# A fused recurrence, gated feed-forward and routed experts on one core: the load order and the step order ahead of the first block are rewritten

## The chip, the cores and the metric

The kernel runs on one core of one Trainium2 chip, in one launch. Its time is the device time of one execution in microseconds (us), the median of three runs. Engines are named as the profile names them: PE is TensorE (matmul), PEld its weight load, DVE is VectorE, ACT is ScalarE, POOL is GpSimd, SP is SyncE, which here only requests transfers ("DMA").

## The reference

Three stages follow each other. Stage one is a decayed linear recurrence over 768 tokens, for 4 batches of 8 heads of size 48:

```
for t in range(S):
    cur = np.einsum('bhd,bhe->bhde', u[None] * kt, vt)
    y[:, :, t] = np.einsum('bhd,bhde->bhe', rt, state + cur)
    state = w[None, :, :, None] * state + np.einsum('bhd,bhe->bhde', kt, vt)
```

Stage two is a gated feed-forward layer on the 3072 x 384 result: `silu(x @ w_gate) * (x @ w_val) @ w_out`, with an inner size of 1536. Stage three sends each token to one of 8 experts (the largest of 8 logits), runs `relu(h @ w1) @ w2` with an inner size of 1024 there, and scales the row by the router's and an output gate's value.

## The kernel before, in words

The tokens are cut into 24 tiles of 128. Tile i of the program is chunk i // 4 of batch i % 4, so that tiles 0, 1 and 2 are the first chunks of three batches and have no earlier state. Three tiles make a block of 384 tokens; there are 8 blocks. `b_block` runs a block through the feed-forward layer, over 12 slices f of its weights: `b_up` (L498, then silu and product in `b_act`) and, two slices later, `b_down` (L517). The recurrence of the next block's tiles, the conversion of the weights and the routing of the block before are put into `slots` between these matmuls. The experts come last.

Everything stands in a `tc.manual_schedule()`: each engine executes its instructions in the order in which the program issues them, and waits where an operand is not ready. The order of the code is thus the order on each engine, SP included. Every load is requested from SP.

The change lies in the prologue, up to the first `b_up`, and these steps are in it:

- `setup_consts`: zeros and masks; the two loads of the rates w into `wT` (L125).
- `decay_tables` (L155 to L169): a chain of small DVE operations on the rates, which makes the tables `WT` and `pw`.
- `a_load_kr(i)`: keys and receptances of tile i with features on the partitions, into `kr3[i]` (spare11, spare10, spare9), as three loads of 48 partitions: 192 KB and twice 96 KB. `kr3[i]` has been zeroed before. `a_load(i)`: r, k and v of the tile with tokens on the partitions, one load of 576 KB.
- `a_scale(i)` (L322, L324; DVE): the keys and receptances times the tables. `a_scores(i)` (L367; PE): 8 products, 128 x 128 each, into two banks.
- `a_bonus(i)` (L328, L329; POOL): r * u * k in place. `a_diag(i)`: DVE sums it per head (L338), then ACT (tiles 0 and 1, L345, 8 instructions) or POOL (tile 2, L347) writes the sums onto diagonals `at`. `a_mask(i)` (L372; DVE): the scores are copied into `at` above the diagonal.
- `a_out_mm(i)` (PE): `at` times v. Pair 3 of the heads comes first (L394); ACT copies its result to `y3` (L401), which each of the pairs 0 to 2 needs for its own L391.
- `a_out_ev(i)`: the result goes to `xT`, as a high part that ACT casts (L414) and the rest that DVE subtracts (L415).
- `key_table`: a POOL product (L173), four transposes on PE, and a copy on ACT (L176) to `Wk`, which `a_keys` (L356; POOL) needs.
- `conv_steps(f)` (L218 to L220; DVE): float64 weights to float32, by three DVE operations for each of three thirds of 384 columns; the thirds of slice 0 are called step 0, 1 and 2 below. `conv_b`: of the converted weights ACT casts the high part (L236) and POOL subtracts the rest (L237); part `GV` are the first two thirds, `OUT` is the third. `gate_a` (L245 on PE, L247 on ACT) transposes the third one.
- `pe_warm(n)`: n matmuls (L149) whose result nobody reads.

After the prologue comes `conv_a(1)`, the conversion of slice 1 (again 9 DVE operations), and then `b_block(0)`. Its matmuls need all three tiles' `xT` and slice 0's weights. The state copies, scans and memsets named in the code are not needed below.

Of the kernel before, what the change touches and what calls it, by code (L numbers as in the profile page):

```python
# [8 lines left out]
F32 = mybir.dt.float32  # L9
# [42 lines left out]
def kernel(  # L52
# [58 lines left out]
    def bc(ap, axis, shape):  # L111
        return ap.unsqueeze(axis).to_broadcast(shape)
# [4 lines left out]

    def setup_consts():
        dve.memset(wT, 1.0)
        dve.memset(rev, 0.0)  # L120
        act.activation(out=rev, in_=rev, func=AF.Silu)
        dve.memset(kr3[0], 0.0)
        pool.memset(kr3[1], 0.0)
        for j in range(2):
            sp.dma_start(  # L125
                out=wT[64 * j : 64 * j + HD, :],
                in_=w_d.rearrange("(p j) d -> j d p", j=2)[j],
            )
        sp.dma_start(out=ub, in_=u_d.rearrange("h d -> (h d)").partition_broadcast(P))
        make_identity(nc, ident)  # L130
        pool.memset(triu, 1.0)
        pool.affine_select(
            out=triu, in_=triu, compare_op=ALU.is_gt, fill=0.0, base=0,
            pattern=[[1, P]], channel_multiplier=-1,
        )
        pool.tensor_copy(out=mask, in_=triu)
        pool.memset(ones, 1.0)
        pool.memset(cnt, 0.0)
        pool.memset(kr3[2], 0.0)
        pool.memset(spare[4][:, 0 : 6 * P], 0.0)  # L140
        for c in range(KC):
            pool.tensor_copy(
                out=shf[:, c].rearrange("s (j m) -> s j m", j=2)[:, :, HD:64],
                in_=ident.rearrange("s (j m) -> s j m", j=2)[:, :, 16 * c : 16 * c + 16],
            )

    def pe_warm(n, b=7):
        for _ in range(n):
# [19 lines left out]
            dve.tensor_tensor(out=pw[:, :, :, b + 1], in0=pw[:, :, :, b], in1=pw[:, :, :, b], op=ALU.mult)  # L168
        dve.tensor_tensor(out=pw[:, :, :, 7], in0=pw[:, :, :, 6], in1=pw[:, :, :, 6], op=ALU.mult)  # L169

    def key_table():
        wk2 = kp.rearrange("s h d -> s (h d)").rearrange("s (p t) -> s p t", p=4)
        pool.tensor_tensor(out=wk2, in0=WkT, in1=bc(pw[:, 0, :, 7], 2, [P, 4, P]), op=ALU.mult)  # L173
        for p in range(4):
            pe.transpose(bank[7][:, p * P : (p + 1) * P], wk2[:, p, :], ident)
        act.copy(  # L176
            out=Wk.rearrange("s (h d) -> s h d", h=NH),
            in_=bank[7].rearrange("s (h d) -> s h d", h=NH)[:, :, 0:HD],
        )
# [117 lines left out]
    def a_load_kr(i):  # L297
# [7 lines left out]
        else:  # L305
            att.setdefault(i, {}).update({"k": krT[:, 0], "r": krT[:, 1]})
            for j in range(2):
                sp.dma_start(out=krT[64 * j : 64 * j + HD], in_=krT_d[n, j])

    def a_load(i):  # L310
        if i < 3:
            rkv = spare[NF - 4 - i][:, 0 : 3 * DM].rearrange("s (a c) -> s a c", a=3)
        else:
            rkv = apool.tile([P, 3, DM], F32, tag="rkv", name="rkv", bufs=2)
# [493 lines left out]

    with tc.manual_schedule():
        setup_consts()  # L810
        for i in range(3):
            a_load_kr(i)
            a_load(i)
        for f in range(3):
            next_w(f)
        sp.dma_start(out=G, in_=g_d)
        decay_tables()
        for b in range(2):
            pool.memset(Sst[b], 0.0)
        a_bonus(0)  # L820
        a_scale(0)
        a_scores(0, 0)
        a_bonus(1)
        a_scale(1, (0,))
        a_diag(0, True)
        a_scale(1, (1,))
        a_scores(1, 2)
        pe_warm(20)
        a_bonus(2)
        a_scale(2)  # L830
        a_diag(1, True)
        a_mask(0, 0)
        a_out_mm(0, 6, (3,))
        a_scores(2, 4)
        a_diag(2, False)
        a_out_mm(0, 6, (0, 1, 2))
        a_mask(1, 2)
        a_mask(2, 4)
        steps = conv_steps(0)
        a_out_ev(0, 6)  # L840
        steps[0]()
        a_out_mm(1, 0, (3,))
        key_table()
        a_out_mm(2, 1, (3,))
        a_out_mm(1, 0, (0, 1, 2))
        steps[1]()
        a_out_mm(2, 1, (0, 1, 2))
        steps[2]()
        a_out_ev(1, 0)
        pool.memset(krT, 0.0)  # L850
        for i in range(3):
            a_keys(i)
        for b in (2, 3):
            pool.memset(Sst[b], 0.0)
        conv_b(0, (GV,))
# [261 lines left out]
def _layout(inputs):  # L1117
# [21 lines left out]
    for i, name in enumerate(("moe_w_gate", "moe_w_val")):  # L1139
# [8 lines left out]
    return {  # L1148
        "krT": np.ascontiguousarray(np.stack([feat(inputs["k"]), feat(inputs["r"])], axis=3)),
        "rkv": np.ascontiguousarray(np.stack([tok(inputs[n]) for n in "rkv"], axis=2)),  # L1150
        "w": np.ascontiguousarray(inputs["w"]), "u": np.ascontiguousarray(inputs["u"]),
        "w64": w64, "g": g, "w12": w12,
    }

# [20 lines left out]
```

## Time and profile before

| | |
|---|---|
| time, three runs | 858.78 us median (857.08 to 859.10) |
| the profiled execution | 857.18 us, of which the span is 855.5 us |
| busy share of the span | PE 96%, PEld 93%, DVE 54%, ACT 32%, POOL 31% |
| granted TensorE clock over the span, as a share of 2.4 GHz | 0.993 |
| HBM traffic over the span | 120 GB/s |

The shares are means over stages that differ. In the first fortieth of the span (21.4 us) the page gives PE 4 tenths and DVE 7, in the second PE 9 and DVE 8. What a change of the prologue is worth is therefore read from the prologue's own rows and from the chain of waits behind it, not from the shares. In the rows below a line number is that of the kernel before.

### The profile page before, as it was taken

How to read it: one execution, taken by the hardware profiler on the slowest of the kernel's cores; microseconds unless marked ns; L12 is line 12 of the kernel's file. 1: busy time of each engine (PE TensorE's matmuls, PEld its weight loads, DVE VectorE, ACT ScalarE, POOL GpSimd, SP SyncE). 2: the span in 40 equal slices, each digit the busy share in tenths (PEclk: the TensorE clock that was granted, in tenths of full speed). 3: DMA queues.
4: the chain of work that ended last, by engine and by line, in shares of the span. 5: the costliest groups of instructions: out<-in, count | busy, mean ns of one | idle time of the engine just before them, and what ended most of it. 6: DMA issues, size and time to landing. Idle time of an engine off the chain costs nothing.

```text
span 855.5 us, 13963 instructions
## 1 busy us (share of the span) xinstructions
PE 824.2 (96%) x5472; PEld 793.4 (93%) x5472; DVE 459.5 (54%) x945; ACT 271.2 (32%) x590; POOL 265.4 (31%) x241
## 2 busy tenths in 40 slices
PE   4988899999999999999999999999999999999996
PEld 3768789999999999999999999999999999999996
DVE  7888764344465455456455444234565566466541
ACT  2334342212211221222222222223454444444432
POOL 6755564233334425244244112010110211021022
PEclk9989999999999999999999999999999999999999
DMA  8815415843333322323323210410494544435201
GB/s 225 303 53 188 154 61 138 238 127 117 102 111 100 122 79 89 117 87 125 114 102 130 61 48 29 162 51 1 140 349 142 170 140 140 157 123 167 82 26 36
DMA packets 29769, 104.90 MB, mean 123 GB/s; under 512 B 5175, under 2 KB 14193, under 8 KB 26624
## 3 DMA queue, kind: packets, MB, share of 16 engines
q1 hardware_dynamic: 26368, 94.37, 34.4%
q0 software_dynamic: 3328, 9.56, 3.0%
q8 instruction: 45, 0.74, 0.4%
q14 instruction: 28, 0.23, 0.1%
HBM read 85.84 MB, written 16.41 MB: 120 GB/s over the span
## 4 chain that ended last, share of the span: by engine, by line
PE 87%; DVE 7%; issue 2%; DMA 1%; ACT 1%; SPq 1%; POOL 0%; POOLq 0%; DVEq 0%; ACTq 0%
PE bank L498 33%; PE bank L517 17%; PE bank L714 12%; PE bank L731 12%; PE bank L367 3%; PE bank L394 2%; PE bank L380 2%; DVE bank L219 2%; DVE bank L218 2%; DVE cv L220 1%; PE bank L679 1%; PE bank L745 1%; DMA spare<-in_krT_dram 1%; PE bank L431 1%; DVE s L507 0%
## 5 line engine op out<-in xcount | busy, mean ns | idle before, releaser
L498 PE MATMUL bank<-xT,W 128*128 128x384 f32 x1728 | 330.8, 341 | 1.1 <-DMA xT<-stage 0.9
L498 PEld LDWEIGHTS bank<-xT,W 128*128 128x128 f32 x1728 | 304.9, 189 | 5.2 <-DMA xT<-stage 1.5
L517 PE MATMUL bank<-W,h 128*128 128x400 f32 x864 | 174.6, 346 | 0.0
L517 PEld LDWEIGHTS bank<-W,h 128*128 128x128 f32 x864 | 154.7, 188 | 0.4 <-DVE h L510 0.2
L509 ACT CAST h<-s 128x384 fp32r<-128x384 f32 x96 | 49.2, 513 | 325.0 <-DVE s L507 325.0
L507 DVE TENSOR_TENSOR s<-s,bank 128x384 f32<-128x384 f32 x96 | 53.2, 554 | 158.1 <-PE bank L498 145.2
L731 PE MATMUL bank<-hd,wf 128*128 128x416 f32 (+1 forms) x576 | 113.8, 344 | 0.0
L731 PEld LDWEIGHTS bank<-hd,wf 128*128 128x128 f32 x576 | 104.3, 188 | 0.7 <-DVE hd L718 0.2
L753 POOL DMA_INDIRECT out_dram<-yo,ix x32 | 34.2, 1067 | 201.4 <-DVE yo L749 175.1
L347 POOL TENSOR_TENSOR at<-ident,a 128x1024 f32<-128x1024 f32 x19 | 36.0, 1896 | 149.0 <-PE bank L498 118.0
L510 DVE TENSOR_TENSOR h<-s,h 128x384 fp32r<-128x384 f32 x84 | 52.9, 630 | 48.6 <-ACT h L509 48.6
L718 DVE SCALAR_TENSOR_TENSOR hd<-bank,hd 128x416 fp32r<-128x416 f32 (+1 forms) x64 | 36.7, 573 | 77.0 <-ACT hd L717 77.0
L663 DVE TENSOR_TENSOR wf<-raw,wf 128x768 fp32r<-128x768 f32 x64 | 61.2, 957 | 7.0 <-ACT wf L662 1.2
L506 ACT ACTIVATE s<-bank 128x384 f32<-128x384 f32 x96 | 47.2, 492 | 46.8 <-PE bank L498 46.8
L579 POOL DMA_INDIRECT xs<-rows,slot x24 | 23.7, 988 | 112.9 <-DVE slot L577 51.5
L717 ACT ACTIVATE hd<-bank 128x416 fp32r<-128x416 f32 (+1 forms) x64 | 32.3, 505 | 82.3 <-PE bank L714 81.9
L714 PE MATMUL bank<-xd1h,wf 128*128 128x416 f32 x192 | 58.3, 361 | 0.0
L662 ACT CAST wf<-raw 128x768 fp32r<-128x768 f32 x64 | 52.8, 825 | 0.0
L372 DVE COPY_PREDICATED at<-mask,bank 128x512 f32<-128x512 int32 x42 | 28.6, 733 | 38.2 <-POOL at L347 35.3
L714 PE MATMUL bank<-xd0h,wf 128*128 128x416 f32 x144 | 43.8, 362 | 0.0
L714 PEld LDWEIGHTS bank<-xd1h,wf 128*128 128x128 f32 x192 | 36.0, 188 | 0.5
L328 POOL TENSOR_TENSOR rkv<-rkv,ub 128x384 f32<-128x384 f32 x21 | 21.3, 1016 | 48.6 <-DMA rkv<-in_rkv_dram 48.6
(177 smaller groups left out, 951.5 us busy)
## 6 DMA issues: line engine op xcount, KB each, us to landing
raw<-in_w_dram SPq DMA_DIRECT2D x36, 768.0 KB, 4.4
raw<-in_w_dram SPq DMA_DIRECT2D x22, 1152.0 KB, 7.2
rkv<-in_rkv_dram SPq DMA_DIRECT2D x21, 576.0 KB, 5.4
krT<-in_krT_dram SPq DMA_DIRECT2D x42, 192.0 KB, 3.4
xs<-zt SPq DMA_DIRECT2D x32, 197.0 KB, 5.8
xr<-xs SPq DMA_DIRECT2D x6, 591.0 KB, 5.7
spare<-in_w_dram SPq DMA_DIRECT2D x2, 1152.0 KB, 9.6
xT<-stage SPq DMA_DIRECT2D x42, 48.0 KB, 2.1
```

Of the source, the lines that this page charges most:

```text
L347: pool.tensor_tensor(out=af, in0=bc(ident, 1, [P, NH, P]), in1=bc(a, 2, [P, NH, P]), op=ALU.mult)
L498: pe.matmul(ps[i], W[f][:, wl, o : o + P], x[:, xl, c, :], start=(c == 0 and n == 0), stop=(c == KC - 1 and n == 2),)
L506: act.activation(out=s, in_=g, func=AF.Silu)
L507: dve.tensor_tensor(out=s, in0=s, in1=v, op=ALU.mult)
L509: act.copy(out=h[:, 0], in_=s)
L510: (pool if blk == 0 else dve).tensor_tensor(out=h[:, 1], in0=s, in1=h[:, 0].bitcast(F32), op=ALU.subtract)
L517: pe.matmul(bank[t][:, 0 : DM + 16], h[:, hl, t * P : (t + 1) * P], W[f][:, wl, 2 * KC * P :], start=(f == 0 and n == 0), stop=(f == NF - ...
L662: act.copy(out=wf[:, 0], in_=raw[:, f])
L663: dve.tensor_tensor(out=wf[:, 1], in0=raw[:, f], in1=wf[:, 0].bitcast(F32), op=ALU.subtract)
L714: pe.matmul(ps, wf[:, wl, c * P : (c + 1) * P], xd[xl][:, c, 0:n], start=(i == 0), stop=(i == 3 * KC - 1))
L718: dve.scalar_tensor_tensor(h[:, 1, 0:n], ps, 0.0, h[:, 0, 0:n].bitcast(F32), ALU.max, ALU.subtract)
L731: pe.matmul(bank[c][:, 0:n], wf[:, wl, o : o + P], h[:, hl, 0:n], start=(f == 0 and i == 0), stop=(f == NEF - 1 and i == 2),)
```

## The change

Loads. The rates come from a second input that the host lays out as 2 x 48 x 4, so that a partition's four values lie together. All nine loads of keys and receptances of tiles 0, 1 and 2 are requested before u and before anything with tokens on the partitions; then r and k of the three tiles (384 KB each, `a_load_part`), weight slice 0, v of the three tiles (192 KB each), slices 1 and 2, and the rest as before.

Zeros. The zeros of `kr3[2]` move from POOL to DVE, ahead of the decay tables; the zeros of two states move ahead of the bonuses on POOL.

Order of the steps. The three bonuses come first, then POOL's product for the key table; the scores of all three tiles are issued before the first `a_out_mm`; 8 dummy matmuls stand in place of 20. The first third of slice 0 is converted before tile 0's `a_out_ev`, the second before tile 1's, the third before tile 2's; `conv_b(GV)` is issued before tile 1's `a_out_ev`, and `gate_a` before tile 2's. The zeros of `krT`, `a_keys` and the last two states' zeros come behind all of this.

```
     def setup_consts():
         dve.memset(wT, 1.0)
+        for j in range(2):
+            sp.dma_start(out=wT[64 * j : 64 * j + HD], in_=wt_d[j])
+        dve.memset(kr3[0], 0.0)
         dve.memset(rev, 0.0)
         act.activation(out=rev, in_=rev, func=AF.Silu)
-        dve.memset(kr3[0], 0.0)
+        a_load_kr(0)
         pool.memset(kr3[1], 0.0)
-        for j in range(2):
-            sp.dma_start(
-                out=wT[64 * j : 64 * j + HD, :],
-                in_=w_d.rearrange("(p j) d -> j d p", j=2)[j],
-            )
-        sp.dma_start(out=ub, in_=u_d.rearrange("h d -> (h d)").partition_broadcast(P))
+        dve.memset(kr3[2], 0.0)
...
-        pool.memset(kr3[2], 0.0)
...
+    def a_load_part(i, lo, hi):
+        t = spare[NF - 4 - i][:, lo * DM : hi * DM].rearrange("s (a c) -> s a c", a=hi - lo)
+        sp.dma_start(out=t, in_=rkv_d[a_tile(i)][:, lo:hi])
+        att[i].update({"rkv"[n] + "n": t[:, n - lo] for n in range(lo, hi)})
...
         setup_consts()
+        a_load_kr(1)
+        a_load_kr(2)
+        sp.dma_start(out=ub, in_=u_d.rearrange("h d -> (h d)").partition_broadcast(P))
         for i in range(3):
-            a_load_kr(i)
-            a_load(i)
-        for f in range(3):
-            next_w(f)
+            a_load_part(i, 0, 2)
+        next_w(0)
+        for i in range(3):
+            a_load_part(i, 2, 3)
+        next_w(1)
+        next_w(2)
         sp.dma_start(out=G, in_=g_d)
         decay_tables()
-        for b in range(2):
-            pool.memset(Sst[b], 0.0)
-        a_bonus(0)
+        for i in range(3):
+            a_bonus(i)
+        key_table_a()
         a_scale(0)
         a_scores(0, 0)
-        a_bonus(1)
-        a_scale(1, (0,))
+        a_scale(1)
+        a_scores(1, 2)
         a_diag(0, True)
-        a_scale(1, (1,))
-        a_scores(1, 2)
-        pe_warm(20)
-        a_bonus(2)
         a_scale(2)
+        a_scores(2, 4)
+        pe_warm(8)
         a_diag(1, True)
         a_mask(0, 0)
         a_out_mm(0, 6, (3,))
-        a_scores(2, 4)
         a_diag(2, False)
+        a_mask(1, 2)
+        key_table_b()
+        a_out_mm(1, 0, (3,))
         a_out_mm(0, 6, (0, 1, 2))
-        a_mask(1, 2)
         a_mask(2, 4)
-        steps = conv_steps(0)
-        a_out_ev(0, 6)
-        steps[0]()
-        a_out_mm(1, 0, (3,))
-        key_table()
         a_out_mm(2, 1, (3,))
         a_out_mm(1, 0, (0, 1, 2))
+        steps = conv_steps(0)
+        steps[0]()
+        a_out_ev(0, 6)
         steps[1]()
+        conv_b(0, (GV,))
         a_out_mm(2, 1, (0, 1, 2))
+        a_out_ev(1, 0)
         steps[2]()
-        a_out_ev(1, 0)
+        gate_a(0)
+        a_out_ev(2, 1)
+        conv_b(0, (OUT,))
         pool.memset(krT, 0.0)
         for i in range(3):
             a_keys(i)
         for b in (2, 3):
             pool.memset(Sst[b], 0.0)
-        conv_b(0, (GV,))
-        a_out_ev(2, 1)
-        gate_a(0)
-        conv_b(0, (OUT,))
```

SP's requests from the third on, before (spare11, 10 and 9 hold the keys of tiles 0, 1 and 2; spare8, 7 and 6 hold their r, k and v):

```order
L129 DMA ub_75<-in_u_dram 128x384
L302 DMA spare11_104<-in_krT_dram 48x1024
L303 DMA spare11_104<-in_krT_dram 48x512
L304 DMA spare11_104<-in_krT_dram 48x512
L315 DMA spare8_101<-in_rkv_dram 128x1152
L302 DMA spare10_103<-in_krT_dram 48x1024
L303 DMA spare10_103<-in_krT_dram 48x512
L304 DMA spare10_103<-in_krT_dram 48x512
L315 DMA spare7_100<-in_rkv_dram 128x1152
L302 DMA spare9_102<-in_krT_dram 48x1024
L303 DMA spare9_102<-in_krT_dram 48x512
L304 DMA spare9_102<-in_krT_dram 48x512
```

The same place in the changed kernel:

```order
L305 DMA spare11_104<-in_krT_dram 48x1024
L306 DMA spare11_104<-in_krT_dram 48x512
L307 DMA spare11_104<-in_krT_dram 48x512
L305 DMA spare10_103<-in_krT_dram 48x1024
L306 DMA spare10_103<-in_krT_dram 48x512
L307 DMA spare10_103<-in_krT_dram 48x512
L305 DMA spare9_102<-in_krT_dram 48x1024
L306 DMA spare9_102<-in_krT_dram 48x512
L307 DMA spare9_102<-in_krT_dram 48x512
L818 DMA ub_75<-in_u_dram 128x384
L315 DMA spare8_101<-in_rkv_dram 128x768
L315 DMA spare7_100<-in_rkv_dram 128x768
```

The keys of tiles 1 and 2 have moved ahead of u and of every load with tokens on the partitions.

DVE from the first scaling on, before (a is the sum for the diagonal of a tile, bank0 and bank1 hold tile 0's scores):

```order
L322 TENSOR_TENSOR spare11_104<-spare11_104,WT_73 128x1024
L324 TENSOR_TENSOR spare11_104<-spare11_104,WT_73 128x512
L322 TENSOR_TENSOR spare10_103<-spare10_103,WT_73 128x1024
L338 TENSOR_REDUCE a_195<-spare8_101 128x4x2
L324 TENSOR_TENSOR spare10_103<-spare10_103,WT_73 128x512
L322 TENSOR_TENSOR spare9_102<-spare9_102,WT_73 128x1024
L324 TENSOR_TENSOR spare9_102<-spare9_102,WT_73 128x512
L338 TENSOR_REDUCE a_238<-spare7_100 128x4x2
L372 COPY_PREDICATED spare8_101<-mask_70,bank0_61 128x512
L372 COPY_PREDICATED spare8_101<-mask_70,bank1_62 128x512
```

The same place in the changed kernel:

```order
L327 TENSOR_TENSOR spare11_104<-spare11_104,WT_73 128x1024
L329 TENSOR_TENSOR spare11_104<-spare11_104,WT_73 128x512
L327 TENSOR_TENSOR spare10_103<-spare10_103,WT_73 128x1024
L329 TENSOR_TENSOR spare10_103<-spare10_103,WT_73 128x512
L343 TENSOR_REDUCE a_210<-spare8_101 128x4x2
L327 TENSOR_TENSOR spare9_102<-spare9_102,WT_73 128x1024
L329 TENSOR_TENSOR spare9_102<-spare9_102,WT_73 128x512
L343 TENSOR_REDUCE a_238<-spare7_100 128x4x2
L377 COPY_PREDICATED spare8_101<-mask_70,bank0_61 128x512
L377 COPY_PREDICATED spare8_101<-mask_70,bank1_62 128x512
```

Tile 1's scaling is no longer cut in two by tile 0's sum; tile 2's stands behind that sum in both kernels.

ACT from the first copy of pair 3 on (bank6, bank0 and bank1 hold the outputs of tiles 0, 1 and 2; cv is slice 0 converted, W0 its parts, gt its transposed third), before:

```order
L401 COPY spare4_97<-bank6_67 48x128 x2
L414 CAST xT_279<-bank6_67 128x3x128
L401 COPY spare4_97<-bank0_61 48x128 x2
L176 COPY Wk_74<-bank7_68 128x384
L401 COPY spare4_97<-bank1_62 48x128 x2
L414 CAST xT_279<-bank0_61 128x3x128
L236 CAST W0_331<-cv_278 128x768
L414 CAST xT_279<-bank1_62 128x3x128
L247 COPY gt_339<-bank7_68 128x384
L236 CAST W0_331<-cv_278 128x384
```

The same place in the changed kernel:

```order
L406 COPY spare4_97<-bank6_67 48x128 x2
L179 COPY Wk_74<-bank7_68 128x384
L406 COPY spare4_97<-bank0_61 48x128 x2
L406 COPY spare4_97<-bank1_62 48x128 x2
L419 CAST xT_296<-bank6_67 128x3x128
L239 CAST W0_302<-cv_292 128x768
L419 CAST xT_296<-bank0_61 128x3x128
L250 COPY gt_322<-bank7_68 128x384
L419 CAST xT_296<-bank1_62 128x3x128
L239 CAST W0_302<-cv_292 128x384
```

The cast of tile 1's output now stands behind the cast of slice 0's first two thirds, and that of tile 2's behind the copy of the transposed third; tile 0's stands behind the copies of pair 3 of all three tiles.

## Rows read from the trace of the kernel before

**Rows 1.** Chain of waits, 25 to 130 us; columns: start us, us, what.

```profile
26.88 0.56 DVE bank L218
...
31.62 0.55 DVE cv L220
...
72.56 2.65 PE bank L498 x9
...
77.51 1.60 PE bank L498 x9
...
111.66 0.56 DVE s L507
```

**Rows 2.** Timeline of DVE; columns: start us, us, instruction, [idle before <-releaser].

```profile
3.50 2.35 DVE L155 TENSOR_SCALAR pw<-wT 128x4 f32<-128x4 f32 x1 [0.81 <-DMA wT<-in_w_dram]
...
9.61 1.22 DVE L322 TENSOR_TENSOR spare<-spare,WT 128x1024 f32<-128x1024 f32 x1
...
13.03 1.40 DVE L322 TENSOR_TENSOR spare<-spare,WT 128x1024 f32<-128x1024 f32 x1 [1.61 <-DMA spare<-in_krT_dram]
14.36 0.54 DVE L338 TENSOR_REDUCE a<-spare 128x8 f32<-128x384 f32 x1
...
17.72 1.23 DVE L322 TENSOR_TENSOR spare<-spare,WT 128x1024 f32<-128x1024 f32 x1 [2.22 <-DMA spare<-in_krT_dram]
...
24.08 1.34 DVE L372 COPY_PREDICATED spare<-mask,bank 128x512 f32<-128x512 int32 x2 [0.76 <-POOL spare L347]
26.40 0.56 DVE L415 TENSOR_TENSOR xT<-bank,xT 128x384 fp32r<-128x384 f32 x1 [0.99 <-ACT xT L414]
...
33.02 0.55 DVE L218 TENSOR_SCALAR bank<-raw 128x384 int32<-128x384 int32 x1
```

**Rows 3.** Timeline of POOL.

```profile
15.63 1.00 POOL L328 TENSOR_TENSOR spare<-spare,ub 128x384 f32<-128x384 f32 x1 [2.28 <-DMA spare<-in_rkv_dram]
16.71 1.00 POOL L329 TENSOR_TENSOR spare<-spare 128x384 f32<-128x384 f32 x1
...
22.15 1.90 POOL L347 TENSOR_TENSOR spare<-ident,a 128x1024 f32<-128x1024 f32 x1 [0.67 <-DVE a L338]
24.00 1.05 POOL L173 TENSOR_TENSOR kp<-WT,pw 128x512 f32<-128x512 f32 x1
```

**Rows 4.** Timeline of SP (a row is a request).

```profile
8.23 0.42 SPq L304 DMA_DIRECT2D spare<-in_krT_dram  x1
```

**Rows 5.** Busy time and DMA by stretch; columns: stretch, length, busy (instructions) of each engine, granted clock, DMA share, GB/s.

```profile
15.00:17.00 2.00, 1.74 (x9) 1.45 (x8) 0.49 (x1) 2.00 (x8) 1.29 (x2) 1.00 1.07 214
18.00:20.00 2.00, 2.00 (x14) 1.22 (x13) 2.00 (x4) 0.00 (x0) 1.09 (x1) 1.00 1.00 417
...
44.00:46.00 2.00, 0.21 (x2) 0.21 (x3) 1.91 (x6) 0.81 (x4) 0.26 (x1) 1.00 0.16 58
...
48.00:50.00 2.00, 2.00 (x9) 2.00 (x9) 1.86 (x4) 0.77 (x3) 2.00 (x1) 0.50 0.00 0
```

**Rows 6.** Timeline of ACT.

```profile
20.04 2.45 ACT L345 ACTIVATE spare<-ident,a 128x128 f32<-128x128 f32 x8 [2.67 <-DVE a L338]
...
27.20 0.53 ACT L401 COPY spare<-bank 48x128 f32<-48x128 f32 x2
29.37 0.48 ACT L414 CAST xT<-bank 128x384 fp32r<-128x384 f32 x1 [1.65 <-PE bank L394]
30.43 0.83 ACT L236 CAST W<-cv 128x768 fp32r<-128x768 f32 x1 [0.57 <-DVE cv L220]
...
32.81 0.48 ACT L247 COPY gt<-bank 128x384 f32<-128x384 f32 x1 [0.64 <-PE bank L245]
```

**Rows 7.** Timeline of PE.

```profile
30.03 0.49 PE L391 MATMUL bank<-spare 128*128 128x128 f32 x2
...
31.22 0.43 PE L394 MATMUL bank<-spare 128*48 128x128 f32 x4
...
32.23 0.55 PE L245 MATMUL bank<-ident,cv 128*128 128x128 f32 x3 [0.58 <-DVE cv L220]
```

More of the change, by code (lines that the diff above doesn't have):

```diff
@@ L57 @@
     w_d: bass.AP,
+    wt_d: bass.AP,
     u_d: bass.AP,
@@ L145, in setup_consts @@
             )
+        for b in range(2):
+            pool.memset(Sst[b], 0.0)
     def pe_warm(n, b=7):
@@ L169, in decay_tables, with key_table_a, key_table_b @@
         dve.tensor_tensor(out=pw[:, :, :, 7], in0=pw[:, :, :, 6], in1=pw[:, :, :, 6], op=ALU.mult)
-    def key_table():
-        wk2 = kp.rearrange("s h d -> s (h d)").rearrange("s (p t) -> s p t", p=4)
+    wk2 = kp.rearrange("s h d -> s (h d)").rearrange("s (p t) -> s p t", p=4)
+    def key_table_a():
         pool.tensor_tensor(out=wk2, in0=WkT, in1=bc(pw[:, 0, :, 7], 2, [P, 4, P]), op=ALU.mult)
+    def key_table_b():
         for p in range(4):
@@ L308, in a_load_kr @@
                 sp.dma_start(out=krT[64 * j : 64 * j + HD], in_=krT_d[n, j])
+    def a_load_part(i, lo, hi):
+        t = spare[NF - 4 - i][:, lo * DM : hi * DM].rearrange("s (a c) -> s a c", a=hi - lo)
+        sp.dma_start(out=t, in_=rkv_d[a_tile(i)][:, lo:hi])
+        att[i].update({"rkv"[n] + "n": t[:, n - lo] for n in range(lo, hi)})
     def a_load(i):
[L311 to L314, printed above, removed]
+        rkv = apool.tile([P, 3, DM], F32, tag="rkv", name="rkv", bufs=2)
         sp.dma_start(out=rkv, in_=rkv_d[a_tile(i)])
@@ L1150, in _layout @@
         "rkv": np.ascontiguousarray(np.stack([tok(inputs[n]) for n in "rkv"], axis=2)),
-        "w": np.ascontiguousarray(inputs["w"]), "u": np.ascontiguousarray(inputs["u"]),
+        "w": np.ascontiguousarray(inputs["w"]),
+        "wt": np.ascontiguousarray(np.asarray(inputs["w"]).reshape(4, 2, HD).transpose(1, 2, 0)),
+        "u": np.ascontiguousarray(inputs["u"]),
         "w64": w64, "g": g, "w12": w12,
```

## Prediction

> **What bounds the kernel now.** I read the chain of waits first, since it tells on which engine the start of the program costs time. From 26.88 us on it runs on DVE, conversion after conversion, and it is still on DVE at 111.66 us [rows 1]. In between it leaves DVE for short pieces on PE, ACT and POOL, each of which follows from a DVE result. So the first block is paced by DVE until about 112 us, and PE only after that. A DVE chain that begins later by x makes the program longer by x, unless one of the short pieces absorbs it. I therefore look for one number: when does DVE begin slice 1's conversion? Now that is at 33.02 us [rows 2]. All that the change does ends ahead of that instruction, and the work behind it keeps its order on every engine but POOL and SP, of which below.
>
> Next I read DVE's timeline ahead of it [rows 2]. The last mask ends at 24.08 + 1.34 = 25.42 us. DVE then waits 0.99 us for tile 0's cast, and from 26.40 us on it does not wait again: tile 0's rest, three conversion steps (26.88 to 32.17 us [rows 1], 1.76 us each), the rests of tiles 1 and 2, slice 1. Ahead of the last mask DVE waits for transfers (1.61 us and 2.22 us for keys [rows 2], POOL 2.28 us for a token tile [rows 3]).
>
> **The loads.** Until 17 us they move at 214 GB/s, from 18 us on at 417 [rows 5]. A key tile (384 KB, three loads of 48 partitions) adds 2.1 us to the stream: tile 1's token load is there at 15.63 us [rows 3], tile 2's keys at 17.72 us [rows 2]. Tile 0's keys are all there by 8.2 us, since SP's request at 8.23 us no longer waits for them [rows 4]. With u (192 KB, about 0.5 us at 417 GB/s) no longer ahead, I take 7.7 us for them, then 9.8 and 11.9 us for tiles 1 and 2. Behind them come u and r, k of tile 0, 590 kB: 1.4 us at 417 GB/s. So r and k of tile 0 land at about 13.3 us, which I call R. Both ends: if the key tiles are held only by SP's requests (0.42 us each [rows 4], say 1.4 us a tile with gaps), R = 7.7 + 2.8 + 1.4 = 11.9 us; if the token loads also go at 214 GB/s, 2.75 us in place of 1.4, R = 14.6 us. I take 13.3 us because a key tile's 2.1 us is measured and nothing of a key load is mixed in any more behind 11.9 us.
>
> The Trainium skill (SBUF — State Buffer, Door 1: The DMA port swizzle) says that a load onto partitions 0 to 47 reaches only 8 of 16 ports, about 218 GB/s at most. The measured 2.1 us for 393 kB is 187 GB/s, of that size; by the page alone a key tile would take 1.8 us, R would be 12.7 us and the sum below 0.6 us smaller. That rule speaks against putting all the slow loads first, since what waits for tokens then stands behind 1.2 MB of them.
>
> Slice 0 (1180 kB) and v follow r, k of three tiles: even v of tile 2 is there by R + 786/417 + 1180/417 + 590/417 = R + 6.1, about 19.4 us, ahead of its use. Fewer packets for the rates bring them at most the 0.81 us earlier that DVE waited for them [rows 2], and DVE is zeroing then. Both cost and gain nothing, as the next paragraph shows; without that cover they would be worth that 0.81 us.
>
> **The steps up to the last mask.** POOL now has three bonuses in a row, 2.08 us each (15.63 to 17.71 us [rows 3]), then the table product (1.05 us) and tile 2's diagonal (1.90 us) [rows 3]; then DVE's last mask (1.34 us [rows 2]). With 0.1 us of gaps the last mask ends at R + 6.25 + 1.05 + 1.90 + 1.34 + 0.1 = R + 10.65, 23.95 us: a gain of 1.5 us at this place. Is DVE ready for it? The second zeroing on DVE, L155 (2.35 us for four columns [rows 2], held by something that the row does not name) and the tables end no later than about 11.1 us (9.61 us now [rows 2], and 1.5 us for a zeroing, an estimate from the width). Two tiles' scalings (1.23 us and about half of it again [rows 2]) end by 14.9 us, before tile 0's bonus at R + 2.1 = 15.4 us lets the first sum go. So anything from a gain of 2.35 us to a loss of 1.5 us there is hidden by the wait for R; without that wait it would shift the masks one for one. The moved zeros on POOL fall before R as well.
>
> Tile 1's mask matters too, for PE waits for it: R + 2.1, sum 0.54 [rows 2], tile 0's diagonal on ACT 2.45, tile 1's 2.45 [rows 6], mask 1.34, 0.1 of gaps: M = R + 9.0 = 22.3 us. The scores of tile 2 (and 8 dummies for 20) lie ahead of this on PE, which is otherwise idle there.
>
> **From there to slice 1.** Here the new order costs. ACT and PE keep program order, and three hand-overs are now in series with DVE's steps, where before only one (0.99 us [rows 2]) was. From M:
>
> - PE: pair 3 of tile 1 (0.43), three pairs of tile 0 (0.81 each: 30.03 to 31.65 us is two), pair 3 of tile 2 (0.43) [rows 7]: M + 3.3. ACT: copies of pair 3 (0.53), then tile 0's cast (0.48) [rows 6]: M + 4.35. DVE finished step 0 at 23.95 + 1.76 = 25.7 us, M + 3.4, and waits about 0.95 us. Its rest for tile 0 takes 0.48 us (26.40 to 26.88 us): M + 4.85.
> - Step 1: M + 6.6. Only then can ACT cast the first two thirds of the slice (0.83 us), and tile 1's cast (0.48 us [rows 6]) stands behind it in ACT's queue: DVE waits 1.35 us for what PE had ready long before. Rest of tile 1: M + 8.45.
> - Step 2: M + 10.2. Now PE transposes the third (0.55 us [rows 7]), ACT copies it (0.48 us), and tile 2's cast (0.48 us [rows 6]) stands behind that copy: DVE waits 1.55 us. Rest of tile 2: M + 12.3.
>
> Slice 1 begins at M + 12.3 = 34.6 us, against 33.02 us: **later by 1.6 us**. The first block's first matmuls need tile 2's cast too and move by about the same. The waits that come (0.95 + 1.35 + 1.55 = 3.85 us, against 0.99 us) outweigh the head's gain. By R's bounds the sum goes from +0.2 us (R = 11.9) to +2.9 us (R = 14.6).
>
> Moved behind on POOL: the zeros of krT, the three key products and two zeros come after slice 0's last rest, from about 36 to 42 us. Queued behind them are tile 3's bonus and slice 1's rest, for which PE's matmuls of slice 1 wait. In the trace PE stands nearly idle from 44 to 46 us (0.21 us busy in 2 [rows 5]) because DVE is behind, so up to some 2 us on PE there is hidden; without that cover it would be 1 to 2 us. SP keeps the later slices' requests behind krT's; slice 3 is converted only in the stretch from 48 us on, and I cost it at nothing.
>
> Against the profiled execution's own 857.18 us (span 855.5) the sum is 858.8 us. That execution lies 1.6 us under the median of the three runs, 858.78 us, so the forecast on the median's scale is **860.4 us**. About 0.3%, 2.6 us, is what a measurement of this kernel can tell from no change.
>
> **Rivals.**
>
> *The features come early and the head wins.* Mechanism: the nine key loads, with nothing mixed in, are limited by SP's requests alone, and R is below 11.7 us, the point from which the sum turns negative. At best DVE's scalings bound the first sum: tables at 8.3 us (1.3 us earlier), two scalings to 12.1 us, then 0.54 + 2.45 + 2.45 + 1.34 + 0.1 = M at 19.0 us and slice 1 at 31.3 us, 1.7 us earlier: 857.1 us. For: the rate from 18 us on. Against: the 2.1 us per key tile. Chance 0.17; faster by over 0.3% only if also the half clock below happens to fall away.
>
> *PE falls to its lower clock in the new gap.* After tile 2's last pair, near M + 8, PE has only three transposes until M + 11.8. In the trace PE was 0.21 us busy from 44 to 46 us, and from 48 to 50 us the granted clock is 0.50, the 1.2 GHz level [rows 5]. Nine matmuls then take 2.65 us against 1.60 us [rows 1]. The first 18 matmuls at that level would be 2.1 us longer, and what follows on PE some more. It decides only where PE's slack behind DVE (about 2 us, above) is used up: with the 1.6 us, 862.5 us. The Trainium skill (TensorE: Matmul & The Clock Gate, What's actually happening) makes the lower clock the state that an idle PE falls back to; the rows of 44 to 50 us agree. Chance 0.23.
>
> *The shift is absorbed.* At 72.56 us the chain lies on nine matmuls at the lower clock [rows 1]. If the later start moves PE's gaps so that this stretch runs at 2.4 GHz, 1.05 us and a little for the transposes come back: 859.1 us, no difference. Chance 0.15.
>
> The forecast itself, with R between the bounds and the chain carried through: 0.45, from 859.0 to 861.7 us.
>
> **How the numbers follow.** Forecast and absorbed shift lie within 0.3% but for the upper end of R (0.07 of slower). The early features lie within it for 0.11 and beyond for 0.06. The clock rival is slower for 0.19 and the same for 0.04. Together: faster 0.06, same 0.68, slower 0.26. The range, 857.5 to 863.0 us, reaches down to 1.3 us under the median of before, into the early features, and up to 4.2 us over it, past the clock rival.
>
> **What would show it.** Right: slice 1's first conversion at 34 to 36 us; DVE idle about 1.4 us ahead of tile 1's rest, released by ACT, and 1.5 us ahead of tile 2's; the last mask near 24 us; POOL's first bonus near 13 us; the DVE chain unbroken to about 112 us. Wrong: the first bonus before 11.7 us, slice 1 before 33 us, or a chain that leaves DVE before 60 us for good.

## The result and the profile after

The changed kernel takes 863.22 us (median of 4 runs, 862.00 to 864.13) against 858.94 us (4 runs, 857.08 to 859.93) for the kernel before, run beside it: ratio 1.0054, 95% interval 1.0037 to 1.0071. It is slower by about 4.3 us. The profiled execution took 862.92 us, its span is 861.1 us, the mean granted clock 0.990.

DVE's timeline of the changed kernel (start, us, instruction, idle time before it and what ended it; line numbers are now 5 higher), to be held against [rows 2]:

```profile
15.37 0.56 DVE L343 TENSOR_REDUCE a<-spare 128x8 f32<-128x384 f32 x1 [3.52 <-POOL spare L334]
15.84 1.53 DVE L327 TENSOR_TENSOR spare<-spare,WT 128x1024 f32<-128x1024 f32 x1
17.29 1.48 DVE L329 TENSOR_TENSOR spare<-spare,WT 128x512 f32<-128x512 f32 x1
...
21.22 1.33 DVE L377 COPY_PREDICATED spare<-mask,bank 128x512 f32<-128x512 int32 x2
23.61 1.34 DVE L377 COPY_PREDICATED spare<-mask,bank 128x512 f32<-128x512 int32 x2 [1.06 <-POOL spare L352]
...
28.27 0.56 DVE L420 TENSOR_TENSOR xT<-bank,xT 128x384 fp32r<-128x384 f32 x1 [1.53 <-ACT xT L419]
...
31.75 0.56 DVE L420 TENSOR_TENSOR xT<-bank,xT 128x384 fp32r<-128x384 f32 x1 [1.28 <-ACT xT L419]
...
35.49 0.56 DVE L420 TENSOR_TENSOR xT<-bank,xT 128x384 fp32r<-128x384 f32 x1 [1.53 <-ACT xT L419]
35.97 0.55 DVE L221 TENSOR_SCALAR bank<-raw 128x384 int32<-128x384 int32 x1
```

Slice 1 begins at 35.97 us, 2.95 us later than before. The three waits ahead of the rests are there, 1.53, 1.28 and 1.53 us. POOL's timeline beside it [rows 3]:

```profile
13.26 1.00 POOL L333 TENSOR_TENSOR spare<-spare,ub 128x384 f32<-128x384 f32 x1 [7.24 <-DMA spare<-in_rkv_dram]
...
16.37 1.86 POOL L334 TENSOR_TENSOR spare<-spare 128x384 f32<-128x384 f32 x1
18.19 1.44 POOL L333 TENSOR_TENSOR spare<-spare,ub 128x384 f32<-128x384 f32 x1
19.71 1.00 POOL L334 TENSOR_TENSOR spare<-spare 128x384 f32<-128x384 f32 x1
```

The bonus products of 1.00 us take 1.86 and 1.44 us where DVE scales tile 2, and the second part of that scaling takes 1.48 us, against 0.68 us for tile 0 at 9.43 us. PE's timeline [rows 7]:

```profile
18.83 3.16 PE L372 MATMUL bank<-spare 128*128 128x128 f32 x14 [0.92 <-DVE spare L329]
21.83 1.46 PE L149 MATMUL bank<-ones 128*128 128x384 bf16 x8
...
24.16 0.42 PE L399 MATMUL bank<-spare 128*48 128x128 f32 x4
...
34.02 0.55 PE L248 MATMUL bank<-ident,cv 128*128 128x128 f32 x3 [2.25 <-DVE cv L223]
35.52 5.02 PE L503 MATMUL bank<-xT,W 128*128 128x384 f32 x18 [0.95 <-ACT xT L419]
...
59.05 0.80 PE L248 MATMUL bank<-ident,cv 128*128 128x128 f32 x3 [3.26 <-DVE at L377]
...
61.71 3.35 PE L522 MATMUL bank<-W,h 128*128 128x400 f32 x9
```

Tile 1's mask ends at 22.55 us, but its pair 3 runs only at 24.16 us. The scores of tile 2 and the 8 dummies lie ahead of it, end 0.74 us behind the mask (21.83 + 1.46 = 23.29 us), and are followed by tile 0's pair 3 and the key table's transposes, 0.94 us together, ahead of tile 1. Busy times by stretch, columns as in [rows 5], show the granted clock:

```profile
18.00:22.00 4.00, 3.17 (x16) 3.09 (x17) 3.74 (x7) 2.85 (x10) 3.92 (x5) 0.57 1.03 426
...
34.00:38.00 4.00, 3.03 (x10) 2.49 (x11) 2.40 (x5) 1.27 (x3) 2.05 (x3) 0.66 0.00 0
...
62.00:66.00 4.00, 4.00 (x13) 3.97 (x13) 2.09 (x4) 0.73 (x3) 1.19 (x3) 0.50 0.19 34
```

PE stands at 1.2 GHz in three stretches (from 18.2, 35.3 and 59.2 us), each behind a wait. The last one lies on the path. The chain of waits of the changed kernel there (L512 is the silu product on DVE):

```profile
57.18 0.56 DVE s L512
...
60.41 1.46 PE bank L256 x6
61.87 3.19 PE bank L522 x9
65.06 2.10 PE bank L503 x9
67.26 0.57 DVE s L512
...
116.67 0.56 DVE s L512
```

and the same pieces of the kernel before:

```profile
54.23 0.55 DVE s L507
...
57.23 0.84 PE bank L253 x6
58.07 1.73 PE bank L517 x9
59.80 1.60 PE bank L498 x9
61.50 0.56 DVE s L507
```

From the first of these products to the second it took 7.27 us and takes 10.08 us. So the chain is 2.95 us late up to 57.18 us and 5.76 us late at 67.26 us. Then it gets 0.75 us back, since the half-clock stretch that lay on the path before (72.56 us in [rows 1]) has gone, and stands at 5.01 us at 116.67 us. There is 0.6 us more by the end of the span.

### The profile page after: what moved, and what is told of

Same layout as the page of the kernel before. It is cut to its first block, busy times and chain, and to the rows that moved or that the text cites. A ratio compares the mean times of both kernels' runs of the same rounds, so it can differ in the third digit from the quotient of the medians.

```text
span 861.1 us, 13942 instructions
## 1 busy us (share of the span) xinstructions
PE 823.8 (96%) x5460; PEld 793.2 (92%) x5460; DVE 458.3 (53%) x946; ACT 270.8 (31%) x590; POOL 266.7 (31%) x240
## 4 chain that ended last, share of the span: by engine, by line
PE 82%; DVE 7%; issue 5%; ACT 2%; POOL 1%; DMA 1%; SPq 0%; POOLq 0%; DVEq 0%
PE bank L503 32%; PE bank L522 17%; PE bank L719 11%; PE bank L736 11%; PE bank L372 3%; PE bank L399 2%; PE bank L385 2%; DVE bank L222 2%; DVE bank L221 2%; DVE cv L223 1%; PE bank L684 1%; PE bank L750 1%; DMA spare<-in_rkv_dram 1%; PE bank L436 1%; POOL W L240 1%
## 5 line engine op out<-in xcount | busy, mean ns | idle before, releaser
L522 PE MATMUL bank<-W,h 128*128 128x400 f32 x864 | 176.0, 348 | 0.0
L522 PEld LDWEIGHTS bank<-W,h 128*128 128x128 f32 x864 | 155.9, 189 | 0.4 <-DVE h L515 0.2
L512 DVE TENSOR_TENSOR s<-s,bank 128x384 f32<-128x384 f32 x96 | 53.2, 554 | 161.6 <-PE bank L503 148.5
L515 DVE TENSOR_TENSOR h<-s,h 128x384 fp32r<-128x384 f32 x84 | 50.7, 603 | 48.6 <-ACT h L514 48.6
L377 DVE COPY_PREDICATED at<-mask,bank 128x512 f32<-128x512 int32 x42 | 28.5, 732 | 38.2 <-POOL at L352 35.3
```

Of the source, the lines that this page charges most:

```text
L512: dve.tensor_tensor(out=s, in0=s, in1=v, op=ALU.mult)
L515: (pool if blk == 0 else dve).tensor_tensor(out=h[:, 1], in0=s, in1=h[:, 0].bitcast(F32), op=ALU.subtract)
L522: pe.matmul(bank[t][:, 0 : DM + 16], h[:, hl, t * P : (t + 1) * P], W[f][:, wl, 2 * KC * P :], start=(f == 0 and n == 0), stop=(f == NF - ...
```

## The experiments

The kernel before ran beside them on the same chip; its medians in the four sessions were 858.61, 858.60, 858.91 and 858.32 us. Each run has 7 to 12 executions, and the one whose trace is shown lies up to 2.8 us from the median of its run (e2 856.88 us, e4 863.09 us), so a trace tells where time goes in one execution, and the table what the edit is worth. "Tail" means the steps from the first `conv_steps` on.

| run | edit | median us | ratio to before, 95% |
|---|---|---|---|
| e1 | before + new tail | 862.30 | 1.0030 to 1.0059 |
| e2 | after, rests not in series | 859.70 | 0.9999 to 1.0028 |
| e3 | before + new loads, zeros | 861.21 | 1.0012 to 1.0040 |
| e4 | after + 18 dummies ahead of slice 3's transposes | 860.58 | 1.0010 to 1.0036 |
| e5 | after, tile 2 scaled early | 860.07 | 1.0001 to 1.0028 |
| e6 | e2 and e5 together | 857.70 | 0.9981 to 1.0006 |
| e7 | e6 + the 18 dummies | 855.98 | 0.9959 to 0.9987 |
| e8 | e3 + 16 dummies ahead of tile 1's scores | 859.13 | 0.9993 to 1.0019 |
| e9 | after + 16 dummies ahead of tile 2's scores | 861.33 | 1.0021 to 1.0048 |
| e10 | e9 + the 18 dummies | 859.51 | 1.0002 to 1.0024 |
| e11 | after, the last hand-over undone | 860.82 | 1.0021 to 1.0049 |
| e12 | e7 with the old load order | 859.67 | 1.0006 to 1.0028 |
| e13 | after, POOL's zeros and keys early | 862.54 | 1.0033 to 1.0067 |
| e14 | e6, POOL's zeros and keys early | 855.72 | 0.9954 to 0.9980 |
| e15 | e7, POOL's zeros and keys early | 857.75 | 0.9981 to 1.0005 |

**The halves of the change apart: the tail (e1), the loads (e3), the rests out of series (e2).** e1 is the kernel before with the tail of the changed one (POOL's zeros and keys late too), but with `key_table` and the out-products where they were. e3 has only the new loads and zeros. e2:

```
         steps[1]()
-        conv_b(0, (GV,))
         a_out_mm(2, 1, (0, 1, 2))
-        a_out_ev(1, 0)
         steps[2]()
-        gate_a(0)
+        a_out_ev(1, 0)
+        conv_b(0, (GV,))
         a_out_ev(2, 1)
+        gate_a(0)
         conv_b(0, (OUT,))
```

> The kernel before with only the new order of the tail of the prologue (conversion steps, casts, transposes, late zeros); loads and scores as before. Theory S (the hand-overs to ACT and PE that stand in series with DVE's conversion steps): slice 1's conversion begins at about 35.1 us instead of 33.0, DVE waits about 1.3 us ahead of tile 1's rest and 1.5 us ahead of tile 2's, and the time is about 861 us, 2.1 over before. Rival C (the loss comes from stretches at TensorE's lower clock that the new head brings): slice 1's start moves by 2 us too, but the time stays within 1 us of before unless a new stretch at half clock shows. Rival L (the load order): no difference, 859 us.

> The changed kernel with tile 1's rest behind the third conversion step and tile 2's cast ahead of the transposes, so that two of the three hand-overs leave DVE's path; all else as changed. Theory S: DVE still waits about 1.5 us ahead of tile 0's rest, then no more; slice 1 begins at about 33.3 us instead of 36.0, and the time is about 2.7 us under the changed kernel, 860.5 us, if the clock's stretches stay as they are. Rival C: slice 1 begins 2.7 us earlier, but the time follows the half-clock stretches: 860 to 863 us. Rival L: no difference to the changed kernel, 863 us.

> The kernel before with only the new loads (keys first, r and k, slice 0, v, rates in few packets) and the moved zeros of the third key tile; the order of all steps as before. Theory S: the first bonus begins at about 13.3 us, the last mask ends at about 24 us, slice 1 begins at 32 to 33 us, time 857.5 to 859 us. Rival L: slice 1 begins later than 33.5 us, and the time is 2 us or more over before.

The tail alone costs 3.7 us on the kernel before, more than the 2.1 us expected: slice 1 starts at 36.17 us, behind waits of 1.43, 1.28 and 1.89 us, and PE is at half clock around 36 and 62 us there too. Taking the series out of the changed kernel gives back 3.5 us. DVE in e2:

```profile
26.08 0.56 DVE L420 TENSOR_TENSOR xT<-bank,xT 128x384 fp32r<-128x384 f32 x1 [0.21 <-ACT xT L419]
...
29.98 1.01 DVE L420 TENSOR_TENSOR xT<-bank,xT 128x384 fp32r<-128x384 f32 x2
30.91 0.55 DVE L221 TENSOR_SCALAR bank<-raw 128x384 int32<-128x384 int32 x1
```

Two of the three waits are gone, the third is 0.21 us, and slice 1 starts 2.1 us ahead of the kernel before, 2.4 us earlier than was expected (in a profile with the first bonus at 12.39 us and the clock at 1.0 throughout the prologue). So the head of the change does gain for DVE, and the series takes more than that. The time does not follow: e2's median is 1.1 us over the kernel before, which its interval does not tell from no change. e3 was a surprise: the loads alone cost 2.6 us, although its first bonus came at 13.49 us, about as in the changed kernel. PE in e3:

```profile
17.11 3.35 PE L367 MATMUL bank<-spare 128*128 128x128 f32 x14 [3.70 <-DVE spare L324]
20.26 4.73 PE L147 MATMUL bank<-ones 128*128 128x384 bf16 x20
```

PE waits 3.70 us for tile 1's second scaling, which stands behind the first sum on DVE. Its clock then falls to 0.50 from 16.1 to 22.9 us, and the scores of tile 2, behind the dummies, end too late for the last mask (27.21 us, after 3.09 us of waiting for PE; 24 us was expected). That led to the runs with dummies.

**PE's clock: e4 (ahead of slice 3's transposes), e8 and e9 (in the prologue), e10 (both).**

```
                     slots[2 * f - 3 + (f == 3)].insert(0, lambda f=f: gate_a(f))
+                    if f == 3: slots[4].insert(0, lambda: pe_warm(18, 0))
...
         a_scale(2)
+        pe_warm(16)
         a_scores(2, 4)
```

The first is e4, the second e9. e8 has `pe_warm(16)` ahead of `a_scores(1, 2)` in e3.

> The changed kernel with 18 dummy matmuls into a free bank where PE is idle from 55.8 to 59.0 us, ahead of slice 3's transposes; nothing else changed. Theory S with the clock as its multiplier: slice 1 still begins at 36.0 us, the granted clock from 59 to 66 us is 1.00 instead of 0.50, the third silu product comes at about 64.5 instead of 67.3 us, and the time is 860.4 us, 2.8 under the changed kernel. Rival, the lower clock of that stretch costs nothing: 863 us.

> The kernel before with the new loads and zeros alone, and 16 dummy matmuls ahead of tile 1's scores, where PE waited 3.70 us and its clock fell to 0.50. Clock theory: the clock is 1.0 until 30 us, tile 2's scores end about 2 us earlier, the last mask near 26 us in place of 28.55 us, slice 1 starts near 34.5 us in place of 36.6 us, time about 859 us. Rival (the load order costs by itself, through the first bonus or the keys): slice 1 at 36 us or later and 861 us.

> The changed kernel with 16 dummy matmuls ahead of tile 2's scores, where PE waits for DVE from 16.0 to 18.8 us and its clock then falls. The collision of DVE and POOL stays. Theory A1 (most of the prologue's excess is PE's half clock): tile 2's scores take 1.9 us in place of 3.16 us, pair 3 of tile 1 starts near 22.6 us in place of 24.16 us, tile 0's rest waits under 0.3 us in place of 1.53 us, slice 1 starts at 34.4 to 34.8 us and the time is about 861.7 us. Theory A2 (most of it is the collision, which makes the last mask 1 us late): slice 1 stays at 35.4 us or later and the time over 862.5 us.

> The same with the 18 dummies ahead of slice 3's transposes too, so that only the hand-overs in series and the collision are left. If the two clock drops are what lies between the forecast of 860.4 us and the measured 863.2 us, slice 1 starts at 34.4 to 34.8 us, the granted clock is 1.0 from 40 to 70 us and the time is 859 to 860.5 us. If not, it stays above 861.5 us.

Work that nobody reads made all four faster than the same kernel without it: e4 by 2.6 us, e8 by 2.1 us, e9 by 1.9 us, and e10 by 1.8 us against e9. With e8, 0.5 us of what the loads alone cost is left, which is not clear of the spread. PE in e9:

```profile
18.72 1.83 PE L372 MATMUL bank<-spare 128*128 128x128 f32 x14 [0.88 <-DVE spare L329]
20.39 1.46 PE L149 MATMUL bank<-ones 128*128 128x384 bf16 x8
...
22.72 0.43 PE L399 MATMUL bank<-spare 128*48 128x128 f32 x4
```

and DVE in e9:

```profile
26.83 0.56 DVE L420 TENSOR_TENSOR xT<-bank,xT 128x384 fp32r<-128x384 f32 x1 [0.20 <-ACT xT L419]
...
34.06 0.56 DVE L420 TENSOR_TENSOR xT<-bank,xT 128x384 fp32r<-128x384 f32 x1 [1.53 <-ACT xT L419]
34.53 0.55 DVE L221 TENSOR_SCALAR bank<-raw 128x384 int32<-128x384 int32 x1
```

The same 14 score matmuls take 1.83 us for 3.16 us, tile 0's rest waits 0.20 us for 1.53 us, and slice 1 starts at 34.53 us. The collision of DVE and POOL is still in e9 (the last mask ends at 24.84 us), so it is not what made slice 1 later than the forecast's 34.6 us. Nor does each execution have this drop. Five traces (the changed kernel, e2, e4, e11, e13) have the same PE work up to tile 0's rest and no dummies ahead of tile 2's scores; the clock falls there in two, the changed kernel and e4. e13 shows what the others do, with slice 1 at 34.42 us:

```profile
26.72 0.56 DVE L420 TENSOR_TENSOR xT<-bank,xT 128x384 fp32r<-128x384 f32 x1 [0.20 <-ACT xT L419]
```

e10 missed one number: its clock was 0.50 once more, from 50.4 to 53.8 us. In that profile the slow work pushes the dummies back and the chain of waits runs through them, so that its 859.5 us still holds some loss. In e4 the 9 matmuls of L522 behind the dummies take 1.88 us for the 3.35 us of the changed kernel, and the chain goes from the first product to the second in 7.25 us for 10.08 us, as in the kernel before (7.27 us). In e9, e11 and e13, which have the gap and no dummies in it, that piece takes 9.85 to 10.19 us. Slice 1 did not begin at 36.0 us in e4's trace but at 38.86 us, with the first bonus at 14.65 us and the drop in the prologue. PE in e4:

```profile
58.52 3.10 PE L149 MATMUL bank<-ones 128*128 128x384 bf16 x18
61.95 0.55 PE L248 MATMUL bank<-ident,cv 128*128 128x128 f32 x3 [0.32 <-DVE at L377]
...
63.76 1.88 PE L522 MATMUL bank<-W,h 128*128 128x400 f32 x9
```

**Tile 2 scaled ahead of the first sum: e5; with the rests out of series: e6; and with the dummies: e7.**

```
         a_scores(1, 2)
-        a_diag(0, True)
         a_scale(2)
         a_scores(2, 4)
+        a_diag(0, True)
```

> The changed kernel with tile 2's scaling and scores issued ahead of tile 0's sum, so that DVE scales tile 2 in its 3.5 us wait for the first bonus and not beside POOL's second and third bonus. Theory A (the extra 1.3 us of the prologue is DVE and POOL slowing each other, and PE running at half clock while it waits for tile 2): every bonus takes 1.00 us a half, the scores of tile 2 are done before 18 us, the granted clock stays at 1.0 up to 30 us, tile 0's rest needs to wait about 1.0 us in place of 1.53, slice 1 starts at 34.2 to 34.9 us (34.6 was the forecast) and the time is 860.5 to 862 us, less by 1.2 us or more than the change. Theory B (the hand-overs in series alone cost all of it): slice 1 stays at 35.5 us or later and the time at 863 us.

> The same with the old tail: tile 1's rest after step 2, tile 2's cast ahead of the gate's transposes. Theory A: no wait over 0.5 us on DVE behind the last mask, slice 1 starts at R + 17.2 us, about 30.5 us, some 2.5 us ahead of the kernel before; the time is 856.5 to 858.5 us, and a granted clock of 0.50 between 50 and 62 us takes back 1 to 1.5 us of the lead. Theory B: like the run without hand-overs alone, 859.7 us, since the collision costs nothing once the waits are gone. Rival C (the lead is lost wherever it comes from, because the block is bound by the loads of the weights): slice 1 starts early and the time is still 858.6 us or more.

> The kernel of the run before with 18 dummy matmuls in PE's idle stretch of about 3 us ahead of slice 3's transposes. Clock theory: the granted clock is 1.0 from 50 to 66 us, the nine matmuls of L522 there take 1.7 us in place of 3.1 us, and the time is 1 to 2 us less than without the dummies, 855.5 to 857.5 us. Rival: the half-clock stretch only moves to another place on the path and the time stays within 0.5 us; or the dummies delay the transposes and the time rises.

e5 is 3.2 us faster than the changed kernel, e6 5.5 us, e7 7.2 us. In e5 slice 1 starts at 33.62 us, earlier than was expected, with 0.23, 1.28 and 1.89 us of waits: the first is filled, the two behind the conversion steps are not. Tile 0's bonus still meets a scaling there (1.18 and 1.32 us), which was not expected. In the profiles of e6 and e7 every bonus product takes 0.99 to 1.01 us, and PE does not stop ahead of tile 2's scores; slice 1 starts at 30.70 and 30.97 us. e6 without dummies has the gap and the slow matmuls behind it:

```profile
54.01 0.55 PE L248 MATMUL bank<-ident,cv 128*128 128x128 f32 x3 [3.27 <-DVE at L377]
...
55.90 3.35 PE L522 MATMUL bank<-W,h 128*128 128x400 f32 x9
```

e7 has neither (0.33 us of waiting, 1.88 us for the nine), and beats the kernel before by 2.6 us. The piece between the two products takes 8.82 us in e6 and 7.25 us in e7.

**One hand-over undone: e11** (`a_out_ev(2, 1)` moved ahead of `gate_a(0)`), **and the old load order under the best steps: e12** (u, then keys and tokens tile by tile).

> The changed kernel with one thing undone: tile 2's cast and rest stand ahead of the transposes of slice 0's third, so that the cast doesn't wait for step 2 through PE and ACT. By the forecast's own term (1.55 us for this hand-over, 1.53 us in the profile) DVE no longer waits there, slice 1 starts at 34.3 to 34.6 us and the time is about 861.7 us. Rival: PE's first 18 matmuls start later by the transposes and the copy behind the cast, and the time stays at 863 us.

> The fastest kernel so far (bonuses first, tile 2 scaled early, no hand-overs in series, 18 dummies) with the loads in the old sequence: keys, then tokens, tile by tile, u ahead of them. If the load order is what lets this order of steps run, DVE waits for tile 2's keys until about 17.7 us with tile 0's sum queued behind, slice 1 starts at 32.5 us or later in place of 30.97 us and the time is 857.5 to 859.5 us. If the loads add nothing, the time is 856 us again.

e11 takes 860.82 us, 2.4 us less. Its profile has no wait ahead of tile 2's rest. It also has the granted clock at 1.0 from 14.5 to 31.6 us with the very same code up to there, so the drop in the prologue is not in each execution, and slice 1 starts at 32.70 us, earlier than was expected. Of the 2.4 us the wait itself is worth 1.5 us; what the rest is stays open, though e11's executions spread from 858.38 to 863.63 us, and a drop that only some of them have would do that. e12 loses 3.7 us against e7. DVE in e12:

```profile
17.52 1.56 DVE L327 TENSOR_TENSOR spare<-spare,WT 128x1024 f32<-128x1024 f32 x1 [1.85 <-DMA spare<-in_krT_dram]
...
35.52 0.55 DVE L221 TENSOR_SCALAR bank<-raw 128x384 int32<-128x384 int32 x1
```

The keys of tile 2 come at 17.5 us with the first sum queued behind them. So the load order is worth something to an order of steps that fills the wait for the tokens. How much of the 3.7 us is the keys alone is not shown: in e12 the clock also falls to 0.50, from 20.7 to 24 us and again near 52 us.

**The moved POOL work: e13 to e15**, which put the zeros of `krT`, `a_keys` and the last zeros ahead of `conv_steps(0)`.

> The changed kernel with the zeros of krT, the key products and the last two zeros back ahead of slice 0's conversion on POOL, which is idle there from 23.6 to 31.4 us. Theory P (late POOL work makes PE's long gap): PE's idle time ahead of slice 3's transposes falls from 3.26 us to under 1 us, the half-clock stretch lies before 56 us and is hidden, and the time is about 861 us. Theory Q (the gap comes from DVE's and PE's own order, and the moved POOL work was hidden, as the prediction had it): the gap stays at 3.0 us or more, the half-clock stretch stays behind it, and the time is within 0.7 us of 863.2 us.

> The kernel with tile 2 scaled early and without hand-overs, no dummies (857.7 us), with the same POOL work early. Theory P: no long gap at 50 to 54 us, time about 856 us as with the dummies. Theory Q: gap 3.27 us and 857.7 us again.

> The fastest kernel (18 dummies, 855.98 us) with the same POOL work early. Theory P: the dummies now have no gap to fill and delay PE, 856.5 us or more. Theory Q: 856.0 us within 0.5 us.

In the changed kernel the move is worth 0.7 us, not clear of the spread, and the gap stays at 3.25 us: theory Q. Without hand-overs it is worth 2.0 us, and with it the dummies cost 2.0 us: the times that theory P gave. PE in e14, the kernel with the lowest median (ratio 0.9967; e7 is 0.3 us above it, which is within the spread):

```profile
43.46 0.55 PE L248 MATMUL bank<-ident,cv 128*128 128x128 f32 x3 [2.29 <-DVE S L450]
...
45.82 2.98 PE L503 MATMUL bank<-xT,W 128*128 128x384 f32 x9
...
53.77 0.55 PE L248 MATMUL bank<-ident,cv 128*128 128x128 f32 x3 [1.74 <-DVE at L377]
...
55.57 2.68 PE L522 MATMUL bank<-W,h 128*128 128x400 f32 x9
```

Here PE's idle time falls ahead of 43.46 us, the clock is 0.50 from 46.1 to 49.5 us, and this slow work still ends before DVE releases the next transposes. In the kernel before PE is at 0.50 from 47.5 to 54.3 us, then waits only 0.18 us, and the clock stays up. In e14 the gap of 1.74 us is left, the clock falls again at 56.4 us, and the piece between the products takes 8.78 us, as in e6 (8.82 us). So theory P is right in the times and has the gap shorter (1.74 for 3.27 us), but the second drop came again in this trace, and where e14's 2.0 us come from stays open.

## Why the prediction was wrong

The forecast was 860.4 us with no measurable change as the likeliest; the time is 863.2 us, just above the range, and slower.

- **Loads: near enough, the exact hit was luck.** R was put at 13.3 us, and the first bonus starts at 13.26 us. Tile 1's scaling at 10.03 us did not wait for its keys, nor did tile 2's in e6 at 11.77 us (forecast 9.8 and 11.9 us). But with the same loads the first bonus starts at 12.39 us in e2 and at 14.65 us in e4, and the stream already moves 387 GB/s from 11 to 12 us, when the forecast had it on the last key tile at 187 GB/s: the keys probably came earlier than forecast, and tile 0's tokens took longer. Of a key tile's three loads only the first goes to partitions 0 to 47, the other two to 64 to 111; from 4 to 10 us, when they run, the stream moves at about 200 GB/s all the same.
- **Hand-overs in series: right.** Forecast 1.35 and 1.55 us ahead of the rests of tiles 1 and 2, measured 1.28 and 1.53 us. e1, e2 and e11 show that they cost; the times moved by more than these waits (3.7, 3.5 and 2.4 us). The price is that of an engine queue: tile 1's cast had its input from PE at about 29.5 us, and ran at 31.25 us behind a cast that waits for step 1.
- **The first step that failed: the scores of tile 2 "lie ahead of this on PE, which is otherwise idle there".** They were taken as covered, which they are at 2.4 GHz: in e9 they and the dummies end at 21.85 us, ahead of the mask. But in the new order they wait for DVE until 18.83 us, PE's clock falls in that wait, and at 1.2 GHz PE comes to tile 1's pair 3 only 1.6 us after its mask (24.16 against 22.55 us). Slice 1 came 1.4 us later than forecast; e9 puts it at 34.53 us, 0.1 us from the sum, and the time back by 1.9 us. With the same PE work up to there the drop is in two of five traces, so it is not in each execution of this kernel either, as far as the traces go.
- **"2.08 us each" for the bonuses failed too, but cost little.** Two of them met DVE's scaling and took 1.3 us more together, so the last mask ended at 24.95 us and not 23.95 us. The wait of 0.95 us that the sum had ahead of tile 0's rest took this up: in e9 it is 0.20 us. What the collision alone is worth once the clock is held was not run.
- **The step that cost most: "a DVE chain that begins later by x makes the program longer by x, unless one of the short pieces absorbs it".** A short piece on PE can also grow. From the first product to the second, 7.27 us became 10.08 us, 2.8 us where the prediction had nothing, because PE had waited 3.26 us there and the chain goes on through PE at 1.2 GHz. With dummies in that wait the piece takes 7.25 us (e4), and the time falls by 2.6 us (e4) and 1.8 us (e10 against e9).
- **The clock rival was the right mechanism at the wrong place.** It was priced on the first 18 matmuls. They did run at half clock (5.02 us from 35.52 us), and this cost nothing: the chain stayed 2.95 us late up to 57.18 us. The stretch that cost lies 25 us further on.
- **The absorbed shift happened**, 0.75 us, and was outweighed.
- **POOL's moved work at nothing: true for this kernel within 0.7 us (e13).** Where the hand-overs are gone, late POOL work costs 2.0 us without the dummies (e6 against e14), and with them it is the early work that costs 1.8 us (e15 against e7).

With dummies against both drops (e10) the changed kernel takes 859.5 us, 0.6 us over the kernel before; the forecast for this case was 1.6 us over. So the sum of the steps up to slice 1 held (34.61 us in e10), and what lay beyond it is PE's clock in two places. Nearly every sign that the prediction named came true, slice 1 at 35.97 us, the two waits, the first bonus, the chain on DVE to 116.67 us, and the time still missed, since none of them looked at PE behind slice 1. Why the long gap lies ahead of slice 3's transposes, where the kernel before waits 0.18 us, is not shown by a run of its own; in the trace of the kernel before PE fills that place with work at half clock.

## What to carry to other kernels

A cast that is ready but queued behind a cast that waits for a conversion step waits for that step too: count, for each reordered cast or copy, what stands ahead of it on its own engine. Wherever a change makes PE wait, price what PE does next at the lower clock, and follow the chain to the next place where it goes through PE, not only to the first matmuls. Requesting the operands of the first products earlier did not pay here with the old order of steps (e3, e8); it paid with one that uses the wait it leaves (e7 against e12).

## What was not expected of the hardware

Two-input operations of DVE and POOL held each other up by whole instructions. POOL's product began at 16.37 us, while DVE's scaling ran until 17.37 us, and ended 0.86 us behind it, at 18.23 us. DVE's next one, from 17.29 us, ended 0.54 us behind the product and took 1.48 us for 0.68 us. Each thus ran nearly its whole length after the other had ended. The trace of the kernel before has it too, beside a DVE scaling of 18.86 to 19.55 us, and the prediction's 2.08 us passed over it:

```profile
18.91 1.49 POOL L328 TENSOR_TENSOR spare<-spare,ub 128x384 f32<-128x384 f32 x1 [1.20 <-DMA spare<-in_rkv_dram]
```

The Trainium skill (SBUF — State Buffer, Who interferes with whom) says that a DVE instruction with two SBUF inputs and a GpSimd instruction that reads SBUF exclude each other for whole instructions; this trace agrees, 1.86 and 1.44 us for 1.00 us.

Adding 18 useless matmuls (3.10 us of PE) made the kernel 1.7 to 2.6 us faster, where PE without them was idle for 3.26 or 3.27 us. The Trainium skill (TensorE: Matmul & The Clock Gate, What's actually happening) has the lower clock as the state of an idle PE that activity releases; e4 and e7 agree, with 1.88 us for nine matmuls where 3.35 us stood. But the same dummies cost 2.0 us in e15, where the gap was 1.74 us (e14). In e15's profile the transposes behind them start at 55.52 us, 1.75 us later than in e14, but the second product only 0.16 us later (60.85 against 60.69 us), so where the 2.0 us of the medians lie is not shown.
